# Moving the start of a weights' pool and of an activations' tile to multiples of 128 bytes

## The chip, the core and the metric

The kernel runs on one core of one Trainium2 chip. Its time is measured on the device in microseconds (us), as the median over several runs. The profile is one execution recorded by the hardware profiler on the same core.

## The reference

Attention over 8 sequences of 576 tokens with 8 heads of 64, each head under a fixed mask, feeds a two-layer network of width 512, 2048, 512 with a sigmoid-approximated GELU:

```python
scores = scale * np.matmul(q, k.transpose(0, 1, 3, 2))
scores = np.where(masks[None, :, :, :], scores, -1000000000.0)
...
attn = np.exp(scores)
attn = attn / (np.sum(attn, axis=-1, keepdims=True) + 1e-09)
return np.matmul(attn, v).astype(np.float32)
...
h = x @ w_in
g = h * (1.0 / (1.0 + np.exp(-1.702 * h)))
return (g @ w_out).astype(np.float32)
```

All tensors are fp32. Half of the heads have a mask of a local window of 32, the other half one of every 32nd position.

## The kernel before

Both matrix products of the network are done by the seven-product scheme for 2x2 blocks (Strassen's, in Winograd's form), and each fp32 operand is split into a rounded part and the rest, both of type fp32r, so that one product of two tiles is three matmuls: high by high, high by low, low by high. Nearly all of TensorE's time is these matmuls, and each of them has its own weight load.

**First stage** (to about 480 us). For each sequence the attention of its heads is computed in small matmuls, and its output goes to `arena`. ScalarE and VectorE split it into `xa` (`x_high`, `x_low`). `product` (line 520) multiplies it by the split first weights, which lie in tiles named `w` of the pool `wp`: six matmuls for a product, stationary operand `w`, moving operand `xa`, 288 columns. `combine` adds the products and stores the result to the DRAM tensor `hid`. The first sequence is done without the seven products, by `unit` (line 495), with the same kinds of operands. That makes 2736 matmuls of 288 columns.

**Second stage** (from about 480 us). For each of 18 sets of 256 tokens and each of 4 parts of the hidden width, `load_g` fetches a piece of `hid` into `arena`, `g_act`, `g_sums` and `g_split` apply the GELU, form sums and split the result into one of three buffers, taken in turn: one is a tile `ga` of the pool `wp`, two lie in `xa`, which is free by then (`ga_views`, line 862). `products` (line 893) issues 42 matmuls for a part, with one of the three buffers as stationary operand and a tile `w_out` of the pool `wp` as moving operand, 256 columns, which `late_w` (line 821) lays out as two runs of 128 columns. That makes 18 x 4 x 42 = 3024 matmuls, a third of them with `ga` and two thirds with `xa`.

Per partition, `arena` (line 105), `xa` (line 129), two tables and `warm` (line 157, a scratch of one element for an early activation) lie one behind the other in the pool `const`; the pool `wp` with nine buffers of 14336 bytes, and `small`, come behind them. Inside these tiles all operands of the large matmuls begin at multiples of 128 bytes from the tile's start, so the start of `xa` and of `wp` sets where each of them begins:

```python
AT_M = AT_H + 6 * HALF
ARENA = AT_M + 5 * HALF
...
    arena = const.tile([P, ARENA], F32, name="arena")
...
    xa = const.tile([P, 7 * 4 * HALF], F32R, name="xa")
...
    wp = ctx.enter_context(tc.tile_pool(name="wp", bufs=FP + 1))
...
    masks_sb = const.tile([P, 5, WL], BF16, name="masks_sb")
    ident_sb = const.tile([P, P], F32, name="ident_sb")
    small = ctx.enter_context(tc.tile_pool(name="small", bufs=3))
...
    warm = const.tile([P, 1], F32, name="warm")
```

The order of the work is written out by hand (a table for the opening, then slots between the products), engine by engine. All DMAs are issued by SyncE. A profile gives line 87, a helper that issues every operation, for nearly all instructions, so groups are told apart by their tiles. A name such as `mx<-w_out,ga` is the output, then the moving operand and the stationary operand.

Of the kernel before, what the change touches and what calls it, by code (L numbers as in the profile page):

```python
# [9 lines left out]
F32 = mybir.dt.float32  # L10
# [8 lines left out]
P = 128  # L19
# [10 lines left out]
HALF = S // 2  # L30
# [20 lines left out]
AT_PT = AT_PR + 2 * PRW  # L51
AT_H = AT_PT + 2 * 512
AT_M = AT_H + 6 * HALF
ARENA = AT_M + 5 * HALF


def _pairs():
# [13 lines left out]
def attn_ffn(ctx, tc, qk, vs, weights, masks, ident, out):  # L71
    nc = tc.nc

    const = ctx.enter_context(tc.tile_pool(name="const", bufs=1))
# [29 lines left out]

    arena = const.tile([P, ARENA], F32, name="arena")

# [47 lines left out]

    pairs = _pairs()

    warm = const.tile([P, 1], F32, name="warm")
    vector.memset(warm, 0.0)
    zeros = mid[0].bitcast(BF16)[:, :512]
    vector.memset(mid[0], 0.0)  # L160
# [931 lines left out]
```

## Time and profile before

| | |
|---|---|
| median of 3 runs | 842.79 us (842.55 to 843.26) |
| span of the profiled execution | 842.3 us |
| median less this span | 0.5 us |
| TensorE matmuls busy | 825.6 us, 98% |
| TensorE weight loads busy | 802.5 us, 95% |
| VectorE, ScalarE, GpSimd busy | 537.7, 420.2 and 484.5 us |
| granted TensorE clock | 0.999 over the span |

The profile gives no time for the profiled execution other than its span, first to last instruction. A matmul's recorded duration is longer than the distance to the next one's start, since they are pipelined; what a matmul costs in a stream is the distance from start to start, which the timeline gives.

### The profile page before, as it was taken

Reading aid. Unit: us, or ns where it says so; the run is one execution under the profiler, and the core shown is the slowest. Engines: PE = TensorE matmul, PEld = TensorE weight load, DVE = VectorE, ACT = ScalarE, POOL = GpSimd, SP = SyncE. Lnnn points to the kernel's source line nnn. Section 1 sums busy time; section 2 is a strip of 40 time slices with the busy share of each in tenths; the row PEclk is TensorE's granted clock in tenths of the full one; section 3 lists DMA queues with packets and bytes.
Section 4 is the critical chain, followed back from the end, with each engine's and each line's share of the span. In section 5 each row is a group of like instructions: output and inputs, shape, how many; then the busy total and the mean of one; then the engine's idle time right before and its main releaser. Section 6 shows DMA issues by size and latency. Waiting matters only on the chain. (4 is left out here: it accounts for less than half of the span.)

```text
span 842.3 us, 23955 instructions
## 1 busy us (share of the span) xinstructions
PE 825.6 (98%) x9816; PEld 802.5 (95%) x9821; DVE 537.7 (64%) x877; ACT 420.2 (50%) x660; POOL 484.5 (58%) x512
## 2 busy tenths in 40 slices
PE   7899999999999999999999999999999999999998
PEld 4799989999999999999999999999999999999997
DVE  5665876867767658677677755666555545554453
ACT  4675534434434434344446556565555555555550
POOL 4633876333442433334426269999877777777770
PEclk9999999999999999999999999999999999999999
DMA  9898675586776776867578944444444344433421
GB/s 346 303 410 287 218 233 182 184 254 221 210 252 203 240 232 191 260 206 227 183 263 249 289 147 150 127 148 153 128 145 128 126 129 143 130 126 126 142 84 51
DMA packets 112510, 164.84 MB, mean 196 GB/s; under 512 B 9744, under 2 KB 88336, under 8 KB 111504
## 3 DMA queue, kind: packets, MB, share of 16 engines
q1 hardware_dynamic: 112400, 163.31, 59.3%
q8 instruction: 77, 1.26, 0.7%
q14 instruction: 33, 0.27, 0.1%
HBM read 104.55 MB, written 58.72 MB: 194 GB/s over the span
## 5 line engine op out<-in xcount | busy, mean ns | idle before, releaser
L87 POOL TENSOR_TENSOR arena<-arena 128x256 f32<-128x256 f32 (+1 forms) x301 | 308.3, 1037 | 155.4 <-ACT arena L87 81.7
L87 DVE TENSOR_TENSOR xa<-arena,xa 128x576 fp32r<-128x576 f32 (+3 forms) x100 | 148.1, 1483 | 97.0 <-DMA arena<-hid 55.0
L87 PE MATMUL my<-xa,w 128*128 128x288 f32 x1128 | 180.7, 300 | 1.4 <-DVE arena L87 1.1
L87 ACT CAST xa<-arena 128x576 fp32r<-128x576 f32 (+3 forms) x103 | 115.2, 1139 | 102.3 <-PE s L87 75.8
L87 PEld LDWEIGHTS my<-xa,w 128*128 128x128 f32 x1128 | 157.3, 189 | 4.6 <-DVE arena L87 2.0
L87 ACT COPY arena<-mx 128x288 f32<-128x288 f32 (+4 forms) x181 | 62.7, 365 | 177.3 <-PE mx L87 142.0
L87 PE MATMUL mz<-xa,w 128*128 128x288 f32 x804 | 131.5, 299 | 0.8 <-POOL xa L87 0.7
L87 PE MATMUL mx<-xa,w 128*128 128x288 f32 x804 | 130.1, 298 | 0.0
L87 DVE TENSOR_TENSOR arena<-my,arena 128x288 f32<-128x288 f32 (+1 forms) x204 | 88.9, 443 | 52.9 <-PE my L87 50.9
L87 ACT ACTIVATE arena<-arena 128x1024 f32<-128x1024 f32 (+2 forms) x120 | 105.3, 877 | 23.5 <-POOL arena L87 13.8
L87 PEld LDWEIGHTS mz<-xa,w 128*128 128x128 f32 x804 | 113.3, 188 | 2.3 <-POOL xa L87 1.0
L87 PEld LDWEIGHTS mx<-xa,w 128*128 128x128 f32 x804 | 113.5, 189 | 0.9
L87 POOL TENSOR_TENSOR arena<-arena,nmax 128x432 f32<-128x432 f32 (+1 forms) x42 | 51.9, 1236 | 94.7 <-DVE nmax L87 91.3
L87 DVE TENSOR_TENSOR ga<-arena,ga 128x1792 fp32r<-128x1792 f32 (+1 forms) x25 | 52.4, 2097 | 53.4 <-ACT ga L87 32.4
L87 DVE TENSOR_TENSOR arena<-mz,arena 128x288 f32<-128x288 f32 (+1 forms) x166 | 70.0, 440 | 25.2 <-PE mz L87 19.4
L87 POOL TENSOR_TENSOR arena<-arena,rinv 96x512 f32<-96x512 f32 (+1 forms) x48 | 48.7, 1016 | 63.2 <-DVE rinv L87 54.4
L87 PE MATMUL mz<-w_out,xa 128*128 128x256 f32 x576 | 75.5, 280 | 0.0
L87 PE MATMUL mx<-w_out,xa 128*128 128x256 f32 x576 | 75.4, 280 | 0.0
L87 PE MATMUL my<-w_out,xa 128*128 128x256 f32 x576 | 75.3, 280 | 0.0
L87 PEld LDWEIGHTS mx<-w_out,xa 128*128 128x128 f32 x576 | 71.1, 188 | 0.0
L87 PEld LDWEIGHTS my<-w_out,xa 128*128 128x128 f32 x576 | 71.0, 188 | 0.0
L87 PEld LDWEIGHTS mz<-w_out,xa 128*128 128x128 f32 x576 | 70.9, 188 | 0.0
(81 smaller groups left out, 1028.0 us busy)
## 6 DMA issues: line engine op xcount, KB each, us to landing
hid<-arena SPq DMA_DIRECT2D x256, 144.0 KB, 3.2
arena<-hid SPq DMA_DIRECT2D x144, 256.0 KB, 3.2
arena<-qk SPq DMA_DIRECT2D x23, 448.0 KB, 4.4
arena<-qk SPq DMA_DIRECT2D x21, 472.0 KB, 5.8
arena<-vs SPq DMA_DIRECT2D x23, 384.0 KB, 4.7
out<-arena SPq DMA_DIRECT2D x34, 256.0 KB, 2.7
stage<-w_out SPq DMA_DIRECT2D x16, 512.0 KB, 4.1
raw<-w_in SPq DMA_DIRECT2D x7, 1024.0 KB, 8.6
```

The costliest lines, as they stand in the source:

```text
L87: ins = call(*args, **kw)
```

## The change

`arena` gets 16 more elements at its end, and `warm` is cut out of a tile of 32 elements instead of one. No element of either addition is read or written.

```diff
 AT_M = AT_H + 6 * HALF
-ARENA = AT_M + 5 * HALF
+ARENA = AT_M + 5 * HALF + 16
...
-    warm = const.tile([P, 1], F32, name="warm")
+    warm = const.tile([P, 32], F32, name="warm")[:, :1]
     vector.memset(warm, 0.0)
```

All five engines issue the same instructions in the same order. The byte at which the tiles begin in each partition:

| | before | beyond a multiple of 128 | after | beyond a multiple of 128 |
|---|---|---|---|---|
| `arena` | 16512 | 0 | 16512 | 0 |
| `xa` | 62656 | 64 | 62720 | 0 |
| `masks_sb` | 94912 | 64 | 94976 | 0 |
| `ident_sb` | 95552 | 64 | 95616 | 0 |
| pool `wp` (`w`, `raw`, `early`, `sums`, `stage`, `ga`, `w_out`) | 96096 | 96 | 96256 | 0 |
| pool `small` | 225120 | 96 | 225280 | 0 |

## Rows read from the trace of the kernel before

**Rows 1.** The profile's page: span, busy time, slices, the chain that ended last.
```profile
span 842.3 us, 23955 instructions
...
PE 825.6 (98%) x9816; PEld 802.5 (95%) x9821; DVE 537.7 (64%) x877; ACT 420.2 (50%) x660; POOL 484.5 (58%) x512
...
PEclk9999999999999999999999999999999999999999
...
PE 43%; DVE 0%; issue 0%; DVEq 0%
```

**Rows 2.** Busy time by stretch: length, then engines with instructions, clock, DMA share, GB/s.
```profile
0.00:20.00 20.00, 14.02 (x419) 9.47 (x425) 11.37 (x34) 9.24 (x19) 8.77 (x25) 1.00 0.92 344
20.00:60.00 40.00, 36.65 (x577) 33.28 (x578) 26.18 (x57) 27.40 (x49) 19.09 (x14) 1.00 0.92 353
60.00:480.00 420.00, 416.66 (x5794) 401.63 (x5793) 299.94 (x584) 192.37 (x434) 185.36 (x202) 1.00 0.72 230
480.00:842.00 362.00, 358.30 (x3031) 358.10 (x3029) 200.17 (x204) 191.21 (x159) 271.27 (x272) 1.00 0.41 130
```

**Rows 3.** TensorE's timeline in the second stage: start us, duration us, names, count.
```profile
614.74 1.60 PE L87 MATMUL mx<-w_out,ga 128*128 128x256 f32 x12
...
619.78 1.57 PE L87 MATMUL mx<-w_out,xa 128*128 128x256 f32 x12
...
629.63 0.64 PE L87 MATMUL mx<-w_out,ga 128*128 128x256 f32 x4
```

**Rows 4.** TensorE's timeline in the first stage, a stretch without interruption.
```profile
437.79 0.95 PE L87 MATMUL mz<-xa,w 128*128 128x288 f32 x6
...
454.44 0.97 PE L87 MATMUL mz<-xa,w 128*128 128x288 f32 x6
```

**Rows 5.** Groups of weight loads by form: count, busy us, mean ns, idle before.
```profile
L87 PEld LDWEIGHTS my<-xa,w 128*128 128x128 f32 x1128 | 157.3, 189 | 4.6 <-DVE arena L87 2.0 <-DVE w L87 0.9 <-issue 0.2
...
L87 PEld LDWEIGHTS mz<-xa,w 128*128 128x128 f32 x804 | 113.3, 188 | 2.3 <-POOL xa L87 1.0 <-DVE arena L87 0.3
L87 PEld LDWEIGHTS mx<-w_out,xa 128*128 128x128 f32 x576 | 71.1, 188 | 0.0
...
L87 PEld LDWEIGHTS my<-w_out,ga 128*128 128x128 f32 x288 | 36.3, 192 | 0.0
```

**Rows 6.** The same view: small weight loads of plain fp32, from `arena` and from `wp`.
```profile
L87 PEld LDWEIGHTS mx<-arena 64*64 64x64 f32 x360 | 11.7, 134 | 2.5 <-ACT arena L87 2.5
...
L87 PEld LDWEIGHTS mx<-early 64*64 64x64 f32 x48 | 1.8, 134 | 2.2 <-DMA early<-qk 1.3 <-issue 0.9
```

**Rows 7.** Groups of elementwise work by form, whole span, same columns.
```profile
L87 DVE TENSOR_TENSOR xa<-arena,xa 128x1792 fp32r<-128x1792 f32 x47 | 100.2, 2131 | 95.9 <-DMA arena<-hid 55.0 <-ACT xa L87 38.4 <-PE s L87 2.4
L87 ACT CAST xa<-arena 128x1792 fp32r<-128x1792 f32 x47 | 79.5, 1691 | 99.8 <-PE s L87 75.8 <-POOL arena L87 24.0
...
L87 DVE TENSOR_TENSOR ga<-arena,ga 128x1792 fp32r<-128x1792 f32 x23 | 49.7, 2163 | 52.7 <-ACT ga L87 31.7 <-DMA arena<-hid 21.0
...
L87 ACT CAST ga<-arena 128x1792 fp32r<-128x1792 f32 x23 | 38.9, 1692 | 49.1 <-PE s L87 37.1 <-POOL arena L87 12.0
```

**Rows 8.** What TensorE waited for in the first 60 us: total us, times, longest.
```profile
PE mx L87 <- DMA early<-qk: 2.0, 2, 1.0
PE mz L87 <- DMA early<-qk: 1.3, 1, 1.3
```

## The prediction

> **What bounds the kernel now.** I read the page first: TensorE's matmuls are busy for 825.6 of 842.3 us, at the full granted clock (2.4 GHz) throughout, and the chain of work that ended last is TensorE's own, over 43% of the span [rows 1]. That share is the whole second stage: from 480 us on no matmul waits for another engine. The table by stretch comes next [rows 2]. TensorE is busy for 416.7 of 420 us from 60 to 480 us and for 358.3 of 362 us from there to the end; of its 17 idle us, 9.3 lie in the first 60 us. VectorE, the next busiest engine of the first stage, has 300 of 420 us there, GpSimd 271 of 362 us in the second. So what counts is how often TensorE can start a matmul, and the timeline shows that. In the second stage a pass of 42 matmuls with stationary operand `ga` goes from 614.74 to 619.78 us, 120.0 ns each; the two passes with `xa` behind it take 9.85 us for 84 matmuls, 117.3 ns each [rows 3]. In the first stage 126 matmuls lie between the two rows shown, 16.65 us, 132.1 ns each, with 32 columns more [rows 4].
>
> The two passes of the second stage differ in nothing but the stationary buffer: same shape, same moving operand, no wait. `ga` begins 32 bytes beyond a multiple of 64, `xa` at a multiple of 64. The weight loads differ in the same way: 192 ns with `ga`, 188 ns with `xa` [rows 5]. That is the one place where the trace of before prices a start address, and it gives **2.7 ns a matmul**.
>
> **The change part by part.** It removes no instruction and adds none. The pad behind `arena` and the wider `warm` cost only space. What moves are start addresses, by group of consumers:
>
> *Second stage, stationary operand `ga`.* It goes from 32 beyond a multiple of 64 to a multiple of 64, as `xa` is already. 1008 matmuls x 2.7 ns = 2.7 us gained, all of it on the chain. Bounds: 0, if the two buffers differ for another reason, and 2.7.
>
> *The other operand.* After this step each large matmul still has one operand at 32 beyond a multiple of 64 by the addresses of before: in the second stage the moving `w_out`, in the first the stationary `w` (there the moving `xa` is at a multiple of 64). The change mends this too, and the trace of before has no matmul of this kind with both operands at multiples of 64. I bound it by the step that I can see. At most it is worth the same again, 2.7 ns; the weight loads make that plausible, since with one operand off they take 188 ns (`xa`) and 188 to 189 ns (`w`), with both off 192 ns [rows 5], so either operand alone seems to cost about the same. At least it is worth nothing: the first step may already take the load out of the way. Nothing in the trace is nearer to one end than to the other, so I take half, 1.35 ns, and keep both ends. For all 3024 + 2736 = 5760 matmuls that is 7.8 us, between 0 and 15.6. Of it 4.1 us come in the second stage and 3.7 us in the first. In the first stage the gain has to pass through the other engines as well: VectorE's 71% leaves it room, and TensorE's waits there are under 4 us in 420 [rows 2], so I let it all through. If the cover went, `combine`'s adds on VectorE would be late next.
>
> *From 64 to 128.* `xa` also goes from a multiple of 64 to one of 128. No two rows compare such starts; I cost it at nothing, and the two ends above hold for it too.
>
> *Elementwise work.* Writing `xa` or `ga` takes ScalarE 1691 and 1692 ns, VectorE 2131 and 2163 ns [rows 7]: no difference on the first, 1.5% on the second, hidden behind TensorE in both stages. The idle time before these groups is waits for `hid` and for TensorE, so nothing is gained there.
>
> *DMAs into `wp`.* `raw`, `early`, `sums` and `stage` land at other addresses. Only in the opening does TensorE wait for such a transfer, 3.3 us in three waits for `early` [rows 8], while the DMA engines are 92% busy [rows 2]. At most those 3.3 us go, at the worst they double; the mean rate there (344 to 353 GB/s) is the highest of the run, so I take nothing.
>
> Sum: 2.7 + 7.8 = 10.5 us off. The profiled span of 842.3 us becomes 831.8; the median of the runs shown lies 0.5 us above the span, so the forecast is **832.3 us**.
>
> Two sentences of the Trainium skill bear on this, and both speak against it. The row first: two passes that differ in the stationary buffer alone differ by 2.7 ns a matmul [rows 3]. The page "SBUF — State Buffer" gives SBUF lines of 16 bytes (section Specifications), and under Operand start alignment treats a start address as a matter of legality. All starts here are multiples of 32 before the change, so by that rule it is worth nothing and the time stays at 842.8 us. The page "TensorE: Matmul & The Clock Gate" says (Part 2, step-by-step) that TensorE reads moving and stationary operands through two independent ports, so that a load takes no read bandwidth from the running matmul; by that, a longer load of `ga` would be hidden, and the trace does not agree, since the start-to-start distance grows with the load.
>
> **The rivals.**
>
> *The two operands disturb each other when they begin at the same place of a line* (slower). The rows of before can be read another way: 192 ns and 120.0 ns belong to the one pair whose operands begin at the same place within 64 bytes (`w_out` and `ga`, both 32), 188 to 189 ns to the two pairs that begin 32 bytes apart [rows 3, 5]. After the change every pair begins at the same place. The place is then the two `xa` passes of the second stage, which would go from 117.3 to 120.0 ns: 2016 x 2.7 ns = 5.4 us more, 848.2 us. If the first stage pays the same on its 2736 matmuls, 7.4 us more, 855.6 us. It decides as soon as the loads with `xa` take 192 ns. For it: the first stage has its stationary operand off by 32 like `ga`, and its loads still take 188 to 189 ns. Against it: a load reads 128 columns and a matmul 256 or 288, so two reads that start at the same place don't stay there. Chance 0.22.
>
> *Only `ga` gains.* The first step is right, the second is worth nothing: 842.8 - 2.7 = 840.1 us. For it: TensorE may be held by something other than addresses once the load is at 188 ns. Chance 0.13.
>
> *The change does nothing that counts.* The 2.7 ns then belong to where the buffers lie, not to a multiple of 64, and the time is 842.8 us. For it: small plain-fp32 loads take 134 ns from `arena` and 134 ns from `early`, which lies in `wp` [rows 6], so there the start shows nothing. This is what the two pages above would have. Against it: the loads of the large matmuls do differ. Chance 0.15.
>
> The forecast keeps 0.50.
>
> **How the numbers follow.** The forecast's own range goes from both ends of the second step: 842.8 - 2.7 - 15.6 = 824.5 us to 842.8 - 2.7 = 840.1 us. The whole range runs from 824 us to 848.5 us: it takes in the forecast, the two middle rivals and the lower half of the slower rival (848.2 us), and leaves out that rival's upper part and a small tail below, under 0.2 together. About 0.2%, 1.7 us, is what a measurement of this kernel can tell from no change; the forecast and the `ga` case (2.7 us) lie beyond it. Faster: 0.50 + 0.13 less a little for a gain that falls short of 1.7 us, 0.62. Same: 0.16. Slower: 0.22.
>
> **What the profile of the changed kernel would show.** Right: the passes with `ga` and with `xa` take the same time, about 116 ns a matmul; loads with `ga` fall from 192 ns to 188 or below; the first stage's stream goes from 132.1 to about 130.8 ns; the second stage shortens by some 6.8 us, the first by 3.7 us; other engines' means stay. The second step is wrong if `xa` passes stay at 117.3 ns and the first stage at 132.1 ns. The whole is wrong if `ga` passes stay at 120.0 ns, and the slower rival holds if the `xa` passes join them there. The allowance for the opening fails if the waits for `early` grow.

## The result: 0.8% slower

The changed kernel takes 849.92 us in the median of four runs (848.64 to 851.34), the kernel before, beside it, 843.02 us (842.55 to 843.32): a ratio of 1.0079, with a 95% interval of 1.0067 to 1.0091. That is 6.9 us more where 10.5 us less were forecast, and 849.9 lies outside the range of 824 to 848.5 us. It lies where the first rival put it, 848.2 to 855.6 us.

The page of the changed kernel, its head, against [rows 1]:

```profile
span 848.4 us, 23955 instructions
...
PE 833.2 (98%) x9816; PEld 811.0 (96%) x9821; DVE 535.7 (63%) x877; ACT 420.1 (50%) x660; POOL 477.8 (56%) x512
...
PE 43%; DVE 0%; issue 0%; DVEq 0%
```

TensorE has the same number of instructions and is busy 7.6 us longer; the other engines are busy as long as before or a little shorter. The chain that ended last is TensorE's, as it was. TensorE's idle time, span less busy time, is 15.2 us where it was 16.7. So TensorE waits no longer; the matmuls themselves take longer. TensorE's timeline in the second stage (start, duration, names, count), against [rows 3]:

```profile
617.40 1.60 PE L87 MATMUL mx<-w_out,ga 128*128 128x256 f32 x12
...
622.44 1.60 PE L87 MATMUL mx<-w_out,xa 128*128 128x256 f32 x12
...
627.48 1.60 PE L87 MATMUL mx<-w_out,xa 128*128 128x256 f32 x12
```

Each pass of 42 matmuls now takes 5.04 us, 120.0 ns a matmul, whichever buffer is stationary. The `ga` pass has not come down to the 117.3 ns of `xa`; the `xa` passes have gone up to the 120.0 ns of `ga`. The weight loads by form (count, busy us, mean ns), against [rows 5], say the same:

```profile
L87 PEld LDWEIGHTS mx<-xa,w 128*128 128x128 f32 x804 | 114.3, 189 | 0.8
...
L87 PEld LDWEIGHTS mx<-w_out,xa 128*128 128x128 f32 x576 | 72.6, 192 | 0.0
...
L87 PEld LDWEIGHTS mx<-w_out,ga 128*128 128x128 f32 x288 | 36.3, 192 | 0.0
```

In the second stage the loads with `xa` as stationary operand have gone from 188 to 192 ns, those with `ga` are where they were; in the first stage, where `xa` is the moving operand, loads take 188 to 189 ns as before. In the first stage an uninterrupted stretch, against [rows 4]:

```profile
438.39 0.96 PE L87 MATMUL mz<-xa,w 128*128 128x288 f32 x6
...
458.38 1.04 PE L87 MATMUL mz<-xa,w 128*128 128x288 f32 x6
```

150 matmuls lie between these rows, 19.99 us, 133.3 ns each, where 132.1 ns stood before. Over the whole first stage the mean distance from start to start, interruptions of 150 ns and more left out, is 133.1 ns against 132.3 ns.

The account of the 6.9 us: in the second stage 2016 matmuls with `xa` x 2.7 ns = 5.4 us. The first matmul of that stage starts at 480.7 us before and 481.3 us after, and the spans end at 842.3 and 848.4 us, so the stage went from 361.6 to 367.1 us, 5.5 us. The rest, about 1.5 us, fits the first stage's 2736 x 0.8 ns = 2.2 us. But the openings of two profiles differ by a microsecond by themselves: the second stage starts at 480.7 us before and at 479.4 us in a kernel below whose first stage runs at the same pace (the pad behind `arena` alone). And in the profile of the changed kernel the granted clock from 20 to 60 us was 0.96 in the mean, so for a part of it at the lower of its two levels (1.2 GHz), where it was 1.00 before [rows 2]:

```profile
20.00:60.00 40.00, 38.01 (x597) 35.00 (x593) 26.84 (x58) 27.34 (x48) 18.51 (x13) 0.96 0.88 339
```

Counted from the 193rd matmul with `w`, near 62 us in both, it is 418.7 us to the second stage before and 419.8 us after, 1.0 us more. So the first stage's part of the 6.9 us is consistent, but not shown by itself. The waits for `early` fell from 3.3 us [rows 8] to 0.7 us in the profile after, a gain within the allowance of the prediction.

### The profile page after: what moved, and what is told of

It reads as the page before. It is cut to its first block, busy times and chain, and to the rows that moved or that the text cites. A ratio compares the mean times of both kernels' runs of the same rounds, so it can differ in the third digit from the quotient of the medians.

```text
span 848.4 us, 23955 instructions
## 1 busy us (share of the span) xinstructions
PE 833.2 (98%) x9816; PEld 811.0 (96%) x9821; DVE 535.7 (63%) x877; ACT 420.1 (50%) x660; POOL 477.8 (56%) x512
## 5 line engine op out<-in xcount | busy, mean ns | idle before, releaser
L87 POOL TENSOR_TENSOR arena<-arena 128x256 f32<-128x256 f32 (+1 forms) x301 | 302.6, 1017 | 165.8 <-ACT arena L87 92.5
L87 DVE TENSOR_TENSOR xa<-arena,xa 128x576 fp32r<-128x576 f32 (+3 forms) x100 | 145.5, 1456 | 103.3 <-ACT xa L87 60.3
L87 PE MATMUL mz<-xa,w 128*128 128x288 f32 x804 | 131.9, 299 | 0.7 <-POOL xa L87 0.7
L87 PEld LDWEIGHTS mz<-xa,w 128*128 128x128 f32 x804 | 113.3, 188 | 2.1 <-POOL xa L87 1.0
L87 PEld LDWEIGHTS mz<-w_out,xa 128*128 128x128 f32 x576 | 72.6, 192 | 0.0
```

Of the source, the lines that this page charges most:

```text
L87: ins = call(*args, **kw)
```

## The experiments

All distances below are the start of the stationary operand less the start of the moving operand, in bytes of a partition. They follow from the addresses of the tiles; modulo 256 they are the same in all 42 matmuls of a pass where nothing else is said. Times per matmul are from start to start in TensorE's timeline; where a run is given one number for a buffer, it is the mean over its 24 passes.

**Which pad does it?** The change has two pads. One alone moves `xa` to a multiple of 128 and leaves `xa` and `w_out` as far apart as before, 96 bytes modulo 256 (32 modulo 64); the other alone leaves `xa` where it was and brings `wp` to the same place.

The first kernel:

```diff
-ARENA = AT_M + 5 * HALF
+ARENA = AT_M + 5 * HALF + 16
```

> Only the pad behind arena: xa begins at a multiple of 128, wp 32 bytes beyond one. Theory A (a matmul is dearer when its two operands begin at the same place within 64 bytes): the pair xa and w / w_out is 32 apart as before the change, so the passes with xa stay at 117.3 ns, those with ga (same pool as w_out) at 120.0 ns, the first stage at 132.1 to 132.3 ns, and the time at that of before, within 0.3%. Theory B (it is xa's own start, at a multiple of 128, that is dear): xa passes go to 120.0 ns and the time goes to that of the full change, about 850 us.

The second:

```diff
-    warm = const.tile([P, 1], F32, name="warm")
+    warm = const.tile([P, 32], F32, name="warm")[:, :1]
```

> Only the wider warm: xa stays 64 bytes beyond a multiple of 128 and wp begins 64 bytes beyond one too; neither begins at a multiple of 128. Theory A: all pairs begin at the same place, so all passes of the second stage take 120.0 ns, the first stage's stream about 133.1 ns, and the time is that of the full change, 849 to 851 us. Theory B: nothing is at a multiple of 128, so xa passes stay at 117.3 ns and the time is that of before or, if w and w_out gain by being at a multiple of 64, below it.

The first took 843.33 us beside 843.43 us before, ratio 1.0001 (0.9991 to 1.0010); the second 849.62 us, ratio 1.0072 (1.0057 to 1.0087). Their timelines in the second stage, the pad behind `arena` first:

```profile
613.40 1.60 PE L87 MATMUL mx<-w_out,ga 128*128 128x256 f32 x12
...
618.44 1.57 PE L87 MATMUL mx<-w_out,xa 128*128 128x256 f32 x12
...
628.29 1.60 PE L87 MATMUL mx<-w_out,ga 128*128 128x256 f32 x12
```

```profile
616.57 1.60 PE L87 MATMUL mx<-w_out,ga 128*128 128x256 f32 x12
...
621.61 1.60 PE L87 MATMUL mx<-w_out,xa 128*128 128x256 f32 x12
...
626.65 1.60 PE L87 MATMUL mx<-w_out,xa 128*128 128x256 f32 x12
```

With `xa` at a multiple of 128 and `wp` at 32 the two `xa` passes take 9.85 us for 84 matmuls, 117.3 ns, as before the change. With `xa` and `wp` both 64 beyond a multiple of 128, none at one, the `xa` pass takes 5.04 us for 42, 120.0 ns. So a start address by itself counts for nothing here: `xa` at 0 and `xa` at 64 each occur with both times. What counts is where the two operands begin relative to each other. Theory B is out, and with it the forecast's reading: in the second kernel, as in the change, both operands are at multiples of 64, and their passes are the dearest.

**At which distances?** The three stationary buffers of the second stage can be shifted one by one, so that one kernel shows three distances. Its first stage is left as it is. (The tiles of the pool are widened by 32 elements, 128 bytes, to make room. So the distances named here hold modulo 128 only: each buffer of the pool now lies 128 bytes modulo 256 off its neighbour, and in some passes all, in some half, in some none of the matmuls have 128 bytes more.)

```diff
-        both = [w_tile("ga")]
-        both += [xa[:, j * WLEN : (j + 1) * WLEN] for j in range(2)]
+        both = [w_tile("ga", 4)]
+        both += [xa[:, j * WLEN + o : (j + 1) * WLEN + o] for j, o in enumerate((20, 24))]
```

> The layout of before, with the three buffers of the second stage's stationary operand shifted so that each begins at another distance from the moving operand w_out: ga by 16 bytes, the first in xa by 48, the second in xa by 64 (modulo 128). Theory A with a line of 64: 64 takes 120.0 ns as 0 does; 16 and 48 lie below 120, near 117.3 ns. Theory A with a line of 128: 64 is below 120.0 too. Theory B (multiples of 128): none of the three begins at a multiple of 128, all stay at 117.3 ns. The first stage is untouched, 132.1 to 132.3 ns.

On the layout of the change, with shifts of 8, 16 and 24 elements:

> The layout of the change (xa and wp at multiples of 128), with the second stage's stationary operand at other distances from w_out: ga by 32 bytes, the first buffer in xa by 64, the second by 96. Theory A with a line of 64: 117.3 ns for ga and for the second buffer in xa, 120.0 ns for the first. With a line of 128: all three below 120.0 ns. Theory B (a multiple of 128 is dear for w_out as moving operand): all three stay at 120.0 ns. The first stage is that of the full change, about 133.1 ns.

The first gave 119.3 ns at 16, 118.0 ns at 48 and 116.5 ns at 64; the second 119.3 ns at 32, 116.7 ns at 64 and 117.4 ns at 96. A line of 64 bytes is out: 64 is the best distance in both runs, not as bad as 0. And 32 alone doesn't restore 117.3 ns. One run of each took 841.46 and 843.05 us.

These means mix two distances each. In the second kernel all matmuls of the first pass shown have `ga` at 32 modulo 256, all of the second have it at 160:

```profile
599.60 1.58 PE L87 MATMUL mx<-w_out,ga 128*128 128x256 f32 x12
...
604.57 1.58 PE L87 MATMUL mx<-w_out,xa 128*128 128x256 f32 x12
...
614.45 1.60 PE L87 MATMUL mx<-w_out,ga 128*128 128x256 f32 x12
...
619.48 1.57 PE L87 MATMUL mx<-w_out,xa 128*128 128x256 f32 x12
```

The first takes 4.97 us, 118.3 ns a matmul, the second 5.03 us, 119.8 ns. Over all passes with one distance, 32 takes 118.2 ns and 160 takes 119.8 to 120.0 ns; in the first kernel 16 takes 118.2 ns and 144 takes 119.9 to 120.0 ns. So the same place is not the only dear one: 144 and 160 cost as much as 0.

A third kernel, for distances of 64, 128 and 192, had two of its buffers overlap by 32 elements, so that part of the activations was overwritten and TensorE waited 92 us for VectorE's writes of `xa`; it took 975 us and says nothing of distances. On the layout of the change, with tiles widened by 64 elements:

```diff
+        both = [w_tile("ga", 32)]
+        both += [xa[:, j * WLEN + o : (j + 1) * WLEN + o] for j, o in enumerate((48, 16))]
```

> The layout of the change with a pool pitch of a multiple of 256 bytes, so that distances hold modulo 256; the second stage's stationary operand lies 128 bytes (ga), 192 (first buffer in xa) and 64 (second) from w_out. Theory C (the two reads disturb each other by their place within 128 bytes: worst at the same place, least half way round): 128 takes 120.0 ns without scatter as 0 does, 64 and 192 about 116.5 ns. Theory D (only the very same place modulo 256 or more is dear): 128 and 192 are both below 118 ns.

**Does the first stage follow the same rule?** Seven slots of `xa`, each shifted to another distance:

```diff
-        xa[:, i * 4 * HALF : (i + 1) * 4 * HALF].rearrange("p (s c n) -> p s c n", s=2, c=2)
-        for i in range(7)
+        xa[:, i * (4 * HALF + 32) + o : i * (4 * HALF + 32) + o + 4 * HALF].rearrange(
+            "p (s c n) -> p s c n", s=2, c=2
+        )
+        for i, o in enumerate((0, 24, 16, 8, 28, 20, 12))
```

> The layout of the change, with the seven slots of xa shifted so that in the first stage the stationary w begins 0, 32, 64, 96, 16, 48, 80 bytes (modulo 128) beyond the moving operand, for the products 0 to 6. The second stage stays at 120.0 ns. Theory C: the first stage depends on the distance as the second does: dearest at 0 (133.1 ns or more), least at 64, by up to 3.5 ns as between 120.0 and 116.5 ns. Rival theory E (with 288 columns a weight load has room to hide, so the place hardly counts): all seven within 1 ns of each other, 132 to 133 ns.

The means of the seven products run from 131.9 ns (80) to 133.7 ns (96), with 133.1 ns at 0 and 132.6 ns at 64 (start to start, interruptions of 150 ns and more left out): a spread of 1.8 ns and no order that I could name. About half of it need not be the distance: before the change, with all seven slots at one distance, the same means run from 131.8 to 132.7 ns. Both theories missed: it is more than 1 ns, and neither 0 is the worst nor 64 the best. One run took 845.59 us. Its second stage held the surprise. The longer `xa` pushed `wp` on by 896 bytes, so `xa` there lay 128 bytes from `w_out` modulo 256, and its passes took 118.6 ns, not 120.0; `ga`, at 0, took 120.0 ns. So 0 and 128 are not the same, and the period is longer than 128.

**A version with all pairs 64 apart modulo 128.** `wp` at a multiple of 128, `xa` 64 beyond one, `ga` shifted by 64 bytes inside its buffer (tiles of the pool widened by 32 elements):

```diff
-    warm = const.tile([P, 1], F32, name="warm")
+    warm = const.tile([P, 16], F32, name="warm")[:, :1]
...
-        both = [w_tile("ga")]
+        both = [w_tile("ga", 16)]
```

> All large matmuls' operands 64 bytes apart modulo 128: wp at a multiple of 128 (warm of 16 elements), xa 64 beyond one as before, ga shifted by 64 bytes in its buffer. Theory C: every pass of the second stage takes about 116.5 ns, so 1008 x 3.5 + 2016 x 0.8 = 5.1 us less than before; the first stage, if it follows, up to 1.5 ns on 2736 matmuls, 4 us less; 834 to 838 us. Theory E: the second stage's 5 us alone, about 838 us. If the gain of 64 in the earlier run came only from the buffers beside it, at 16 and 48, ga and xa stay at 117.3 ns and the time is 840 us.

It took 836.95 us (836.74 to 838.29 over five runs) beside 843.36 us, a ratio of 0.9925 (0.9912 to 0.9939): 6.4 us faster than the kernel before and 13 us faster than the change. In the profile the second stage goes from 480.9 us to the end of the span at 836.2 us, 355.3 us where it took 361.6 before, so the gain lies there. Its passes:

```profile
612.39 1.52 PE L87 MATMUL mx<-w_out,ga 128*128 128x256 f32 x12
...
617.15 1.57 PE L87 MATMUL mx<-w_out,xa 128*128 128x256 f32 x12
...
622.10 1.56 PE L87 MATMUL mx<-w_out,xa 128*128 128x256 f32 x12
...
627.00 1.57 PE L87 MATMUL mx<-w_out,ga 128*128 128x256 f32 x12
...
631.94 0.28 PE L87 MATMUL mx<-w_out,xa 128*128 128x256 f32 x1
```

The pass from 612.39 us takes 4.76 us, 113.3 ns a matmul; the one from 617.15 us 4.95 us, 117.9 ns; the third 116.7 ns; the one from 627.00 us 117.6 ns. The first and the fourth have the same stationary buffer at the same distance, 192 modulo 256 in each of their matmuls, and differ by 4.3 ns. So do passes that are wholly at 64: 18 of them take 113.3 to 113.9 ns, 12 take 117.8 to 117.9 ns. So from here on the distance modulo 256 alone doesn't give the time.

**Is it 64 modulo 256?** With a pool pitch that is a multiple of 256 the distance is 64 modulo 256 in every matmul of the second stage. The kernel above, with tiles widened by 64 elements in place of 32:

```diff
-        t = wp.tile([P, WLEN + 32], F32R, tag="w", name=name, bufs=FP + 1)
+        t = wp.tile([P, WLEN + 64], F32R, tag="w", name=name, bufs=FP + 1)
```

> As the run with all operands 64 bytes apart, but with a pool pitch that is a multiple of 256 bytes, so that the second stage's stationary operand is 64 bytes beyond the moving one modulo 256 in every matmul (before, half of the weights' buffers made it 192). Theory F (the period is 256: locked at 120.0 ns at distance 0, least, 113.4 ns, at 64, about 117.7 ns at 192 and 118.7 ns at 128): all passes take 113.4 ns, 3024 x about 2.7 ns = 8 us less than that run, 828 to 831 us. Theory C (period 128): 64 and 192 are the same, so the passes stay at about 116.1 ns and the time at 837 us.

Theory F was at odds with the kernel above already, whose passes have both times at 64 and at 192. The run did something that no theory had: seven runs of the same program fell at two places, four at 827.1 to 829.3 us and three at 840.4 to 842.5 us. The profiled run was one of the latter, and all of its passes took 117.8 ns:

```profile
617.57 1.58 PE L87 MATMUL mx<-w_out,xa 128*128 128x256 f32 x12
...
622.52 1.58 PE L87 MATMUL mx<-w_out,xa 128*128 128x256 f32 x12
...
627.47 1.58 PE L87 MATMUL mx<-w_out,ga 128*128 128x256 f32 x12
```

Two passes in 9.90 us, 117.9 ns. Were they all at the 113.3 to 113.4 ns that the kernel above shows in some passes, 3024 x 4.4 ns = 13.3 us would go, which is the distance of the two places. The same program once more:

> The same kernel as the one 64 bytes apart modulo 256, whose runs fell at two places, 827 to 829 us and 840 to 842 us. Theory H (at this distance the stream has two rhythms that hold themselves, one of about 113.4 ns and one of 117.8 ns, and how the stage starts decides which): runs lie at the same two places and at none between, 3024 x 4.4 ns = 13 us apart; a profile of a run at 827 us shows 113.4 ns in every pass, one of a run at 841 us 117.8 ns in every pass. Rival (something outside the second stage, such as the clock or a transfer, makes 13 us): the passes are alike in both, and the difference lies before 480 us or in the granted clock.

One run at 827.73 us, three at 841.3 to 842.5 us. The profiled one was again at the upper place, with 117.8 ns in every pass. The two places are confirmed, and the granted clock does not tell them apart (0.997 to 1.000 at both). That the lower one is the rhythm of 113.4 ns is worked out, not seen in a profile, so the rival, that the 13 us lie outside the second stage, is not ruled out by a measurement.

At other distances, on the layout of the change, with the same pitch and without overlap:

```diff
+        both = [w_tile("ga", 32)]
+        both += [xa[:, j * WLEN + o : (j + 1) * WLEN + o] for j, o in enumerate((8, 48))]
```

> The layout of the change, pool pitch a multiple of 256 bytes; the second stage's stationary operand 128 bytes (ga), 32 (first buffer in xa) and 192 (second) beyond w_out modulo 256, each in every matmul of its pass. Theory F: about 118.7, 118.2 and 117.7 ns. Theory C: 120.0 ns at 128, below 119 at 32, 116.5 ns at 192. The buffers do not overlap; the earlier run with 64, 128 and 192 had two that did, and measured nothing.

```profile
614.93 1.59 PE L87 MATMUL mx<-w_out,ga 128*128 128x256 f32 x12
...
619.92 1.58 PE L87 MATMUL mx<-w_out,xa 128*128 128x256 f32 x12
...
624.88 1.52 PE L87 MATMUL mx<-w_out,xa 128*128 128x256 f32 x12
...
629.64 1.58 PE L87 MATMUL mx<-w_out,ga 128*128 128x256 f32 x12
```

128 takes 118.8 ns here (118.7 ns in the mean), 32 takes 118.1 ns (118.2), 192 takes 113.3 ns in this pass and 117.8 ns in others (115.6). The run took 843.00 us. 128 is not 0, so theory C is out; and 192 has the two rhythms as 64 has, so theory F, which gave each distance one time, is too simple here too.

**The first stage at one distance.** In the first stage the halves of an `xa` slot are 1152 bytes apart, so the distance alternates by 128 modulo 256. With rows of 1280 bytes it is 64 in every matmul:

```diff
-    xa = const.tile([P, 7 * 4 * HALF], F32R, name="xa")
+    xa = const.tile([P, 7 * 4 * 320], F32R, name="xa")
...
-        xa[:, i * 4 * HALF : (i + 1) * 4 * HALF].rearrange("p (s c n) -> p s c n", s=2, c=2)
+        xa[:, i * 4 * 320 : (i + 1) * 4 * 320].rearrange("p (s c n) -> p s c n", s=2, c=2)[:, :, :, :HALF]
...
-    warm = const.tile([P, 1], F32, name="warm")
+    warm = const.tile([P, 48], F32, name="warm")[:, :1]
...
-        both += [xa[:, j * WLEN : (j + 1) * WLEN] for j in range(2)]
+        both += [xa[:, j * WLEN + 32 : (j + 1) * WLEN + 32] for j in range(2)]
```

> The layout of before with the rows of xa in the first stage 1280 bytes apart in place of 1152 (5 x 256), so that the distance of stationary from moving operand is 64 modulo 256 in every matmul of the first stage; in the second stage the xa passes are at 64 too, ga at 0. Elementwise writes of xa take two runs of 288 in place of one of 576. Theory F, if the first stage follows the same rule: its stream falls by up to 6 ns from 133.3 ns, to 127 to 130 ns, 6 to 15 us off the first stage. Theory E (32 more columns give the load its room): 132 ns, the first stage unchanged. Second stage: xa passes 113.4 ns, ga 120.0 ns.

```profile
437.62 0.96 PE L87 MATMUL mz<-xa,w 128*128 128x288 f32 x6
...
454.42 0.96 PE L87 MATMUL mz<-xa,w 128*128 128x288 f32 x6
```

126 matmuls in 16.80 us, 133.3 ns: as in the changed kernel, whose first stage alternates between 0 and 128. So a fixed distance of 64, the best in the runs above, does not help the first stage. Theory F does not carry over; theory E, which had 132 ns and no change, comes nearer but misses by 1.2 ns. Nor is it the single distance that counts there: in the kernel with all pairs 64 apart modulo 128, where the first stage alternates between 64 and 192, its mean is 132.2 ns, where it was 132.3 ns before the change. In the second stage `ga` took 120.0 ns as expected, and `xa`, at 64, took 117.8 ns throughout. One run took 844.65 us.

**Is it the load beside the matmul?** In the changed layout only the low parts of the `xa` operands are moved, 64 bytes away:

```diff
-        both += [xa[:, j * WLEN : (j + 1) * WLEN] for j in range(2)]
-        for i, t in enumerate(both):
-            gv[i] = t.rearrange("p (a k s n) -> p a k s n", a=2, k=7, s=2)
+        gv[0] = both[0].rearrange("p (a k s n) -> p a k s n", a=2, k=7, s=2)
+        for j in range(2):
+            t = xa[:, j * 4032 : (j + 1) * 4032]
+            gv[1 + j] = t.rearrange("p (a k s n) -> p a k s n", a=2, k=7, s=2)[:, :, :, :, :P]
```

> The layout of the change with the low parts of the stationary operand in xa 64 bytes apart from w_out modulo 128, the high parts still at 0; ga (both parts at 0) as control. Theory G (what disturbs is the load of the next stationary operand beside the running matmul, by the pair of their starts): of three matmuls one has such a load apart, and the xa passes fall to about two thirds of the way from 117.7 to 120.0 ns, 118 to 119.5 ns, with a pattern of three; ga stays at 120.0 ns. Rival (the whole stream is held by its worst pair): xa passes stay at 120.0 ns.

```profile
615.91 1.59 PE L87 MATMUL mx<-w_out,ga 128*128 128x256 f32 x12
...
620.94 1.58 PE L87 MATMUL mx<-w_out,xa 128*128 128x256 f32 x12
...
625.90 1.59 PE L87 MATMUL mx<-w_out,xa 128*128 128x256 f32 x12
...
630.88 1.36 PE L87 MATMUL mx<-w_out,ga 128*128 128x256 f32 x10
```

The `xa` passes take 118.1 and 118.4 ns in the mean, `ga` 119.8 ns, so the stream is not held by its worst pair. But the single distances show no pattern of three, and the rows of 144 elements also put the high parts at 128 modulo 256 in turn with 0, which in the kernel with `ga` at 128 is worth 1.3 ns by itself. So this run rules out the rival and does not single out the load. It took 846.46 us.

## Why the prediction was wrong

**What held.** TensorE's own pace was the bound, and neither DMAs nor elementwise work had a part in the result: ScalarE writes `xa` in 1691 ns before [rows 7] and in 1691 ns after. The place where the trace prices an address was the right one, the two kinds of passes in [rows 3], and the price was right: 2.7 ns a matmul is what 2016 matmuls paid, 5.4 us.

**The step that failed.** "*The other operand*" took the four cases (stationary on or off a multiple of 64, moving on or off) as a sum of two costs. The trace had three of them: off and off 192 ns and 120.0 ns, on and off 188 ns, off and on 188 to 189 ns [rows 5]. A sum predicts that on and on is the cheapest. A rule of same or different predicts that it is as dear as off and off. The trace could not tell them apart, and I gave the sum 0.50 and the rule 0.22. The change itself fills the fourth case, and the sum fails there: on and on takes 192 ns and 120.0 ns. The two single pads then show that it is not the multiple of 128: same place 120.0 ns, 96 bytes apart 117.3 ns, whatever the multiples. The term of -7.8 us was +5.4 us in the second stage and, as the remainder, some 1.5 us in the first.

**The first term** failed for the same reason: `ga` shares a pool with `w_out`, so the distance between the two is 0 in any layout that moves the pool as a whole, and the -2.7 us could not come. A gain came only where `ga` was moved inside its buffer.

**My argument against the rival** was that two reads which start at the same place don't stay there, since one reads 128 columns and the other 256. It does not hold against the runs: at distance 0 the matmuls of a settled pass take 120 ns each, so whatever sets the pace there repeats from one matmul to the next. At 96 the single ones lie between 115 and 120 ns.

**The rival** had the place and the price of the second stage right. Its line of 64 bytes was wrong (64 apart is not dear), and "the same place" is only one of the dear distances (144 and 160 are as dear). It over-charged the first stage: 7.4 us were its upper end, 1.2 ns a matmul in an uninterrupted stream and 0.8 ns in the mean are what came, 2.2 us. With 288 columns the products' means lie within 1.8 ns of each other, and not in the second stage's order. Why is open.

**Of the Trainium skill's two sentences,** the lines of 16 bytes ("SBUF — State Buffer", Specifications) stood in the prediction for a change that is worth nothing, and the trace does not agree: the starts are all multiples of 32, and the time moves by 0.8%. The Trainium skill's page "TensorE: Matmul & The Clock Gate" has the load not take read bandwidth from the running matmul (Part 2, step-by-step). The runs show a start-to-start distance that depends on the places of the two operands, which independent ports by themselves would not give; whether the load slows the matmul or the matmul the load, they don't show. The prediction's remark that the start-to-start distance grows with the load holds for the rows of before, but not in general: in the passes at 160 the load takes 188 ns and a matmul 119.8 ns.

**What stays open.** Why at 64 and 192 modulo 256 the stream has two rhythms, 113.3 and 117.8 ns, and what decides which of them a pass or a run takes. The kernel with `ga` shifted has both in one run and is steady from run to run; the one at 64 throughout keeps one rhythm for a whole run. Since one program falls at two places, its addresses alone do not decide it. A profile at 827 us was not caught.

## What to carry to other kernels

Where each matmul has its own weight load and the stream has no other wait, the start of the stationary operand relative to the moving one is a parameter worth trying: here it moved the time from 849.9 us (the same place) over 843 us (in the second stage two thirds of the pairs 96 bytes apart) to 837 us (all 64 apart modulo 128) with no instruction more or less. Rounding every buffer to the same multiple puts all pairs at the same place, and no distance tried with 256 columns was worse. Pad them apart and measure which distance pays, since 144 and 160 were no better than 0; and look at the second operand too, when both come from one pool. And where a trace shows three cases of a two-by-two table, a sum and a rule of same or different fit it equally well: a kernel with the fourth case tells them apart, and here the pad at `warm` alone makes one.

## What the runs showed of the hardware that was not expected

- At distance 0 modulo 256 a matmul of 256 columns with its weight load takes 120.0 ns without scatter in a settled pass; the load shows 192 ns, where other distances show 188 to 190 ns. A matmul of 288 columns takes 133.3 ns in a settled stretch with 0 and 128 in turn, and also with 64 throughout.
- Time of a matmul of 256 columns by distance modulo 256, from passes in which it is the same in every matmul: 0: 120.0 ns, 16: 118.2 ns, 32: 118.2 ns, 48: 117.9 ns, 64: 113.3 to 114.2 or 117.8 ns, 96: 117.3 ns, 128: 118.7 ns, 144: 119.9 ns, 160: 119.8 ns, 176: 118.2 ns, 192: 113.3 or 117.8 ns, 224: 116.8 ns. The values at 16, 48, 144, 160, 176 and 224 come from one profile each.
- The fastest rhythm, 113.3 ns, is 6.7 ns below the slowest; over the second stage's 3024 matmuls that is 20 us, 2.4% of the kernel.
- One program on one core can fall at two places 13 us apart from one run to the next, with a granted clock of 0.997 to 1.000 at both.
